# A searched order written anew: first fills on the rounded identity, first scores planned at half of TensorE's clock

## The chip, the cores and the metric

The kernel runs on one core of a Trainium2 chip. The metric is the device time of one execution in microseconds (us). Before the change it is 619.45 us, the median of three runs (618.64 to 619.97 us).

## The reference

Eight batches, eight heads, 576 positions, head dimension 64. Attention is causal by blocks of 64 positions; its output, 512 wide, goes through a gated feed-forward network with a convolution of three taps along the sequence:

```python
scores = scale * np.matmul(q, k.transpose(0, 1, 3, 2))
scores = np.where(block_i >= block_j, scores, -1000000000.0)
scores = scores - np.max(scores, axis=-1, keepdims=True)
attn = np.exp(scores)
attn = attn / (np.sum(attn, axis=-1, keepdims=True) + 1e-09)
x = np.matmul(attn, v)                    # heads side by side: (8, 576, 512)
h = np.maximum(x @ w_in, 0.0)             # w_in 512 x 1024
conv_out[s] = sum over k of conv_w[k] * h[s + k - 1]
out = (h / (1.0 + np.exp(-conv_out))) @ w_out   # w_out 1024 x 512
```

## The kernel before

The work is built as a list of 3694 operations (`Plan.op`, the class `Plan`), each with an engine, a planned duration, dependencies and buffers, and in some cases other engines on which it may run (`other`). `Plan.order` (L278) then makes the instruction streams. The list `TARGETS` (L21) has one number x per operation: x // 4 is its place on its engine, x % 4 picks one of the engines that it may run on (0 is the first). The operations of each engine are sorted by place; an engine issues its operations in that order and each waits for what it needs, on the chip as in the plan. The plan also gives every operation a start, by planned costs, and two things follow from those starts: which of the eight PSUM banks an operation gets, and where TensorE gets fills. A fill (`work`, L1767; the matmuls are line L1774) is a run of matmuls with a 128x512 result that nothing reads; the plan puts as many of them as fit where TensorE would be idle for more than 0.4 us. `speed` in `order` gives the factor on a TensorE duration, 1.0 at the full clock and 2.0 at half, by the work that the plan placed just before.

The first batch is done in pieces, because the weights arrive meanwhile. Its four head pairs first do queries 0 to 255 (part A: `stage_sa`, scores L1333, mask L1337, row maxima on VectorE L1351, exponentials on ScalarE L1359, norm on GpSimd L1374), then queries 256 to 575 (part B: `stage_sb`, scores L1272, mask L1276, maxima L1288, exponentials L1291; `last_s`, L1120, L1126). The attention weights are turned by TensorE (L1407, copies L677) and multiplied with v (L1451). A feed-forward pass (`ffn`) follows each part: input products L1544, relu L1563 or L1566, taps L1569, L1573, L1577, gate L1589, L1592, two fp16 planes L1599 and L1603, output products L1637, L1647.

The network's weights come as 64-bit words and are decoded, 512 KB at a time, sixteen times: L882 (ScalarE), L885 (GpSimd or VectorE), L889, L892, L897 (VectorE), the maximum L920, and a split into two fp16 planes, L952 and L960 (`wih`, `wil`, `woh`, `wol`).

From the second batch on a head pair goes through `stage_s` (scores L1108, maxima L1207, exponentials L1210), `two_planes` (L1053: the normed weights as a high and a low fp16 plane, L1057, L1063, L1067, L1073, L1079, on VectorE, ScalarE or GpSimd), three or four transposes by DMA (`xbar`, L1095, on SP's queue), and `pair_pv` (products with v, L1491, evacuation L1496, L1499, L1502).

At the start, the constant `rident` (L643, an identity rounded to fp32r) is made on VectorE from `ident`, `blank` (L664) is a 128x128 tile of zeros, and the other constants are made on ScalarE (L647). The first fill multiplies `blank`, all later ones `rident`. `scale_q` (L1015 on GpSimd, L1018 on ScalarE) scales q as it arrives. In the plan TensorE is free from 1.1 us on.

```python
        x = rident if len(fills) > 1 else blank
            return 1.0 if full else 2.0
```

Of the kernel before, what the change touches and what calls it, by code (L numbers as in the profile page):

```python
# [18 lines left out]
PE, DVE, ACT, POOL, SP = 0, 1, 2, 3, 4  # L19

TARGETS = """  # L21
# [199 lines left out]
class Plan:  # L221
# [56 lines left out]
    def order(self, targets, fill, clock):  # L278
        work, slots, unit, least, spare = fill
        step, up, down, begin, switch = clock  # L280
        used, full, known, rows = {}, False, 0, False
# [37 lines left out]
        free = [1.1, 0.0, 0.0, 0.0, 0.75]  # L319
# [1548 lines left out]
```

## Time and profile before

| | |
|---|---|
| three runs, us | 618.64, 619.45, 619.97 |
| profiled execution, us | 621.78 |
| its span, us | 619.9 |
| PE, DVE, ACT, POOL busy, us | 597.5, 530.7, 481.6, 386.9 |
| mean granted TensorE clock | 0.997 |
| fills (L1774) | 89 matmuls, 24.8 us on `rident` and 2.5 us on `blank` |

The span is the time from the first to the last instruction of the profiled execution; 1.88 us lie around it. Matmuls are pipelined and their durations overlap, so "busy" on PE counts the time in which at least one is under way. Fills count as busy. A stage's rows say more than the shares of the whole: the engines have different loads in the first 160 us and after.

### The profile page before, as it was taken

The page shows a single profiled execution, that of the slowest core. Times are in us where ns is not written, and L with a number is a line of the kernel's source. Part 1 is how long each engine was busy: PE and PEld are TensorE (multiplying, and loading weights), DVE is VectorE, ACT ScalarE, POOL GpSimd, SP SyncE. Part 2 cuts the span into 40 slices and gives each one's busy share as a digit, 9 for nine tenths or more (in the row PEclk, how much of TensorE's full clock was granted, in tenths as well). Part 3 has the DMA queues.
Part 4 walks back from the last instruction along what each step waited for, and adds up shares of the span by engine and source line. Part 5 has one row for each costly group of instructions (what it writes and reads, how often), then busy time and mean ns, then how long its engine had stood idle before and what let it go on. Part 6 is the DMA issues. An engine that isn't in the chain of part 4 may idle for free.

```text
span 619.9 us, 15505 instructions
## 1 busy us (share of the span) xinstructions
PE 597.5 (96%) x5832; PEld 381.2 (61%) x5832; DVE 530.7 (86%) x1122; ACT 481.6 (78%) x1234; POOL 386.9 (62%) x496
## 2 busy tenths in 40 slices
PE   8998899979999999999999999999999999999997
PEld 5556454447765477655775567555765667566754
DVE  5999999999889988999999998889889966973850
ACT  5999997796798659997799767978888857962721
POOL 4876665664495846986597454787786617852440
PEclk9999999999999999999999999999999999999999
DMA  8584412799938997699997699459886880594002
GB/s 296 206 293 146 139 35 92 170 224 192 255 78 217 195 221 129 139 196 218 198 189 139 143 223 227 110 116 209 188 172 117 195 145 18 108 163 120 1 1 86
DMA packets 205503, 97.77 MB, mean 158 GB/s; under 512 B 185308, under 2 KB 187636, under 8 KB 205428
## 3 DMA queue, kind: packets, MB, share of 16 engines
q1 hardware_dynamic: 203556, 93.63, 67.1%
q10 hardware_dynamic: 1872, 3.15, 1.8%
q8 instruction: 46, 0.75, 0.5%
q14 instruction: 29, 0.24, 0.1%
HBM read 41.44 MB, written 9.44 MB: 82 GB/s over the span
## 4 chain that ended last, share of the span: by engine, by line
PE 62%; DVE 25%; ACT 6%; POOL 3%; issue 2%; DMA 2%; DVEq 0%; ACTq 0%; POOLq 0%
PE banks L1637 22%; PE banks L1544 21%; PE banks L1491 8%; PE banks L1108 8%; DVE su L1207 3%; DVE t L1573 2%; PE banks L1774 2%; DVE ptbm L1063 2%; DVE t L1592 1%; DVE shared L897 1%; DVE ptbl L1063 1%; DVE st L1288 1%; DVE shared L892 1%; DVE vb L831 1%; DVE h L1063 1%
## 5 line engine op out<-in xcount | busy, mean ns | idle before, releaser
L1637 PE MATMUL banks<-woh,shared 128*128 128x512 f16 (+1 forms) x592 | 184.8, 374 | 0.3 <-DVE t L1592 0.3
L1544 PE MATMUL banks<-x,wih 128*128 128x288 f16 (+2 forms) x1024 | 156.7, 286 | 2.0 <-DVE t L1592 1.8
L1637 PEld LDWEIGHTS <-shared 128*128 128x128 f16 x888 | 82.7, 98 | 100.7 <-issue 15.0
L1544 PEld LDWEIGHTS <-wih 128*128 128x128 f16 x1024 | 98.0, 98 | 36.5 <-issue 8.6
L1207 DVE TENSOR_REDUCE su<-banks 128x1 f32<-128x192 f32 (+8 forms) x252 | 110.8, 478 | 3.1 <-PE banks L1108 2.2
L1637 PE MATMUL banks<-wol,shared 128*128 128x512 f16 (+1 forms) x296 | 110.5, 373 | 0.0
L1586 POOL TENSOR_TENSOR t<-t,shared 128x575 f32<-128x575 f32 x51 | 74.8, 1468 | 54.1 <-DVE t L1573 46.7
L1603 POOL TENSOR_TENSOR shared<-t,shared 128x576 f16<-128x576 f32 (+2 forms) x59 | 71.8, 1219 | 26.0 <-DVE shared L1599 12.8
L1544 PE MATMUL banks<-x,wil 128*128 128x288 f16 (+2 forms) x512 | 86.3, 286 | 0.6 <-DVE wil L960 0.6
L1108 PE MATMUL banks<-k,q 64*64 64x192 f32 (+9 forms) x1120 | 82.7, 414 | 3.9 <-DVE t L1592 1.1
L1491 PEld LDWEIGHTS <-vb 128*64 128x64 f16 x1848 | 63.0, 113 | 11.6 <-issue 10.9
L1573 DVE SCALAR_TENSOR_TENSOR t<-banks,cwb,t 128x575 f32<-128x575 f32 (+2 forms) x72 | 53.0, 742 | 12.5 <-ACT t L1569 7.5
L1108 PEld LDWEIGHTS banks<-k,q 64*64 64x64 f32 x1120 | 42.5, 132 | 33.9 <-issue 12.1
L1589 ACT ACTIVATE t<-t 128x576 f32<-128x576 f32 (+2 forms) x72 | 45.1, 629 | 23.1 <-POOL t L1586 16.5
L1544 PEld LDWEIGHTS <-wil 128*128 128x128 f16 x512 | 49.3, 98 | 14.9 <-DVE wil L960 1.2
L1592 DVE SCALAR_TENSOR_TENSOR t<-t,banks 128x576 f32<-128x576 f32 (+2 forms) x72 | 48.7, 680 | 8.4 <-ACT t L1589 7.6
L1569 ACT ACTIVATE t<-banks,cwb 128x576 f32<-128x576 f32 (+2 forms) x72 | 49.0, 684 | 6.6 <-DVE banks L1566 5.2
L1563 ACT ACTIVATE banks<-banks 128x576 f32<-128x576 f32 (+2 forms) x53 | 30.2, 574 | 15.8 <-PE banks L1544 15.4
L1210 ACT ACTIVATE p3f<-banks,su 128x512 f32<-128x512 f32 (+1 forms) x56 | 36.7, 659 | 5.5 <-DVE su L1207 2.2
L1582 ACT ACTIVATE shared<-banks,cwb 128x575 f32<-128x575 f32 x51 | 37.6, 738 | 1.9 <-DVE t L1573 0.8
L1647 ACT ACTIVATE stage<-banks,osc 128x512 f32<-128x512 f32 (+1 forms) x29 | 19.3, 668 | 24.7 <-PE banks L1637 24.7
L1210 ACT ACTIVATE p2f<-banks,su 128x384 f32<-128x384 f32 (+1 forms) x56 | 30.8, 552 | 8.3 <-DVE su L1207 4.4
(206 smaller groups left out, 1186.9 us busy)
## 6 DMA issues: line engine op xcount, KB each, us to landing
k<-in_k_dram SPq DMA_DIRECT2D x28, 368.0 KB, 3.7
vn<-in_v_dram SPq DMA_DIRECT2D x32, 320.0 KB, 3.9
q<-in_q_dram SPq DMA_DIRECT2D x28, 320.0 KB, 3.7
out_dram<-stage SPq DMA_DIRECT2D x24, 256.0 KB, 2.9
shared<-in_moe_w_in_dram SPq DMA_DIRECT2D x8, 512.0 KB, 4.1
shared<-in_moe_w_out_dram SPq DMA_DIRECT2D x8, 512.0 KB, 3.7
out_dram<-stage ACTq DMA_DIRECT2D x11, 256.0 KB, 3.7
k<-in_k_dram SPq DMA_DIRECT2D x4, 240.0 KB, 4.8
```

The source lines that it names most:

```text
L1108: nc.tensor.matmul(out[64 * y:64 * y + 64], t["q"].ap[64 * r:64 * r + 64, q0:q0 + 64], t["k"].ap[64 * r:64 * r + 64, k0:k0 + c1 - c0], sta ...
L1207: nc.vector.tensor_reduce(out=st.ap[:, k:k + 1], in_=home[hh].ap[:, x], op=ALU.max, axis=AX.X, negate=True)
L1210: nc.scalar.activation(out=y.ap[:, 0:n], in_=home[hh].ap[:, x], func=AF.Exp, bias=st.ap[:, k:k + 1], accum_out=st.ap[:, 9 + k:10 + k])
L1491: nc.tensor.matmul(y, vb.ap[:, w, c, j, :], x, start=first, stop=(z == 1 and c == jobs[-1][0]), skip_group_check=True)
L1544: nc.tensor.matmul(h(a, z), wt[:, c, fs], xs[c][xi].ap[:, x0 + a:x0 + z], start=(n + c - c0 == 0), stop=(n + c - c0 == 3 * NCC - 1))
L1569: nc.scalar.activation(out=t.ap[:, 0:no], in_=h(own, own + no), func=AF.Copy, scale=cwb.ap[:, NFC + f:NFC + f + 1])
L1573: nc.vector.scalar_tensor_tensor(out=t.ap[:, i0:no], in0=h(own + i0 - 1, own + no - 1), scalar=cwb.ap[:, f:f + 1], in1=t.ap[:, i0:no], op0 ...
L1586: nc.gpsimd.tensor_tensor(out=t.ap[:, 0:i1], in0=t.ap[:, 0:i1], in1=u.ap[:, 0:i1], op=ALU.add)
L1589: nc.scalar.activation(out=t.ap[:, 0:no], in_=t.ap[:, 0:no], func=AF.Tanh)
L1592: nc.vector.scalar_tensor_tensor(out=t.ap[:, 0:no], in0=t.ap[:, 0:no], scalar=1.0, in1=h(own, own + no), op0=ALU.add, op1=ALU.mult)
L1603: eng.tensor_tensor(out=g[1][:, f, carry:carry + no], in0=t.ap[:, 0:no], in1=g[0][:, f, carry:carry + no], op=ALU.subtract)
L1637: nc.tensor.matmul(fb.ap[:, 0:cut], g[a][:, f, cs], w[:, f, ds], start=(f == 0 and n == 0), stop=(f == NFC - 1 and n == 2))
```

## The change

`TARGETS` is replaced: all 3694 numbers are written anew; 283 operations get another engine than before, the rest another place or the same. The first fill multiplies `rident` like all others. In the plan alone, which decides bank numbers and fills, TensorE is free from 1.9 us instead of 1.1, `rounded_identity` costs 1.9 us instead of 2.45, everything that starts on TensorE up to 8.5 us has the factor 2.0 of half the clock, and the first three `stage_sa` score operations have a planned duration of 0.95 us for each of their two tiles instead of 0.405, before that factor. `firstk`, which nothing used, becomes `cold`, which counts these operations.

```diff
 TARGETS = """
-0 0 4 8 16 0 4 24 28 12 16 44 64 52 129 80 196 92 185 88 181 252 140 104 280 288 448 8 12 9 4 12 16 8 40 13 32 36 20 64 44 52 44 56 96 40 200 60 60 88
...
+0 4 8 16 0 0 4 24 28 12 20 44 76 52 181 72 240 104 185 96 193 268 152 108 288 296 388 8 20 28 4 8 12 12 44 14 32 40 16 36 32 40 32 40 88 36 184 48 93
...
+    COLD = 8.5
+
     def order(self, targets, fill, clock):
...
-            return 1.0 if full else 2.0
+            return 1.0 if full and t > self.COLD else 2.0
...
-        free = [1.1, 0.0, 0.0, 0.0, 0.75]
+        free = [1.9, 0.0, 0.0, 0.0, 0.75]
...
-    kept, gate, firstk = {}, [], []
+    kept, gate, cold = {}, [], []
...
-    made = [pl.op(DVE, 2.45, rounded_identity, -80.0)]
+    made = [pl.op(DVE, 1.9, rounded_identity, -80.0)]
...
         o = None
+        cold.append(at)
         for tiles in ABLK:
-            o = pl.op(PE, (0.345 + 0.06 * APM) * len(tiles), mm(tiles), at, deps=ready[0] + ready[1] + [o] + made[:2],
+            o = pl.op(PE, (0.95 if len(cold) < 4 else 0.345 + 0.06 * APM) * len(tiles), mm(tiles), at, deps=ready[0] + ready[1] + [o] + made[:2],
...
-        x = rident if len(fills) > 1 else blank
+        x = rident
```

Sorted by engine and place, the new numbers read as follows at the start (old order in brackets). SP: q and k of pair 0, the taps, q of pair 2, a block of weights, k of pair 2, q and k of pair 1 (old: k of pair 2 before the weights). TensorE: scores of part A of pairs 0, 2 and 1, then the turn of the taps (old: the turn before the third scores). ScalarE scales the first q (old: GpSimd), GpSimd the q of pair 2 (old: ScalarE). VectorE, after the maxima of the first scores: shift, maximum and merge of the first weight block, and only then the maxima of the second scores (old: maxima of the second scores first); three more decoding steps of weight blocks 0 and 1 stand ahead of the first part B maximum. Up to the last plane operation that VectorE does for the fourth pair of the second batch, it has 342 operations instead of 352: of the twenty that are no longer among them eleven run on GpSimd, six on ScalarE and three come later; of the ten that are new there, eight were GpSimd's, one ScalarE's and one came later. TensorE changes between score, v-product and other matmul operations 182 times instead of 195: up to the product with v of that fourth pair 53 times instead of 61, after it 129 instead of 134. The position of that product in TensorE's order, the 220th operation, is the same.

## Rows read from the trace of the kernel before

**Rows 1.** Page, engines: busy us, share of the span, instructions

```profile
PE 597.5 (96%) x5832; PEld 381.2 (61%) x5832; DVE 530.7 (86%) x1122; ACT 481.6 (78%) x1234; POOL 386.9 (62%) x496
```

**Rows 2.** Windows: length, busy of PE, PEld, DVE, ACT, POOL; clock, DMA share, GB/s

```profile
14.00:60.00 46.00, 41.80 (x320) 27.52 (x317) 45.81 (x125) 45.69 (x133) 32.99 (x48) 1.00 0.65 228
100.00:137.00 37.00, 32.32 (x308) 16.30 (x298) 34.98 (x91) 30.14 (x89) 22.26 (x33) 1.00 0.68 150
137.00:160.00 23.00, 22.91 (x292) 18.28 (x293) 20.34 (x46) 14.14 (x47) 11.08 (x17) 0.93 1.17 234
160.00:340.00 180.00, 176.45 (x1822) 112.06 (x1820) 168.08 (x329) 153.72 (x388) 130.29 (x156) 1.00 0.84 176
```

**Rows 3.** Chain of waits, 14 to 60 us and 100 to 137 us, by line

```profile
by line: DVE shared L892 14.7%; DVE shared L897 14.2%; DVE st L1288 13.6%; DVE wil L960 11.2%; DVE wm L920 9.0%; DVE shared L889 8.5%; DVE st L1126 4.7%; DVE x L1461 4.5%; issue 3.6%; DVE st L1351 1.7%; DVE t L1577 1.7%; DVE t L1573 1.7%; D
by line: DVE su L1207 16.7%; DMA ptbx<-ptbl 13.7%; DVE ptbl L1063 7.0%; DVE ptbm L1063 6.8%; DVE t L1573 5.3%; DVE t L1592 4.9%; POOL shared L1603 4.3%; DVE h L1063 3.9%; DVE t L1577 2.8%; issue 2.7%; ACT t L1589 2.6%; ACT shared L1596 2.6%
```

**Rows 4.** Chain of waits, single pieces: start us, us, what

```profile
8.08 2.00 PE banks L1774 x4
11.94 0.88 PE banks L1774 x2
138.51 3.85 PE banks L1491 x66
142.36 3.40 PE banks L1774 x14
149.24 2.24 PE banks L1491 x66
157.30 2.26 PE banks L1491 x66
```

**Rows 5.** Timeline of PE, first 13 us: start, us, line [idle before <-releaser]

```profile
1.05 2.50 PE L1774 MATMUL banks<-blank 128*128 128x512 f32 x5 [1.05 <-DVE blank L664]
3.92 0.80 PE L1333 MATMUL banks<-k,q 64*128 64x128 f32 x4 [0.36 <-POOL h L1148]
5.94 0.80 PE L1333 MATMUL banks<-k,q 64*128 64x128 f32 x4
10.02 0.80 PE L1333 MATMUL banks<-k,q 64*128 64x128 f32 x4
12.96 1.13 PE L1272 MATMUL banks<-k,q 64*128 64x512 f32 x4
```

**Rows 6.** Timeline of DVE: maxima and one decoding step in the first 15 us

```profile
5.88 1.35 DVE L1351 TENSOR_REDUCE st<-banks 128x1 f32<-128x256 f32 x4 [0.79 <-PE banks L1337]
7.89 0.76 DVE L1351 TENSOR_REDUCE st<-banks 128x1 f32<-128x256 f32 x2 [0.67 <-PE banks L1337]
9.18 0.66 DVE L892 SCALAR_TENSOR_TENSOR shared<-shared 128x512 int32<-128x512 int32 x1
11.98 1.35 DVE L1351 TENSOR_REDUCE st<-banks 128x1 f32<-128x128 f32 x5 [1.34 <-PE banks L1337]
14.15 0.69 DVE L1288 TENSOR_REDUCE st<-banks 128x1 f32<-128x512 f32 x1 [0.49 <-PE banks L1276]
```

**Rows 7.** Timeline of POOL: the scaling of pair 1's q; and windows, 5 to 8 us

```profile
7.78 0.40 POOL L1015 TENSOR_SCALAR q<-q 128x256 f32<-128x256 f32 x1 [3.95 <-DMA q<-in_q_dram]
...
5.00:8.00 3.00, 2.90 (x19) 1.95 (x17) 1.44 (x6) 1.67 (x8) 0.22 (x1) 1.00 1.00 344
```

**Rows 8.** One line, L1603, 160 to 320 us: ns min/median/max, first and last start

```profile
L1603 POOL TENSOR_TENSOR shared<-t,shared x16: 1272/1282/1863, 171.5 to 319.3; 128x576 f16<-128x576 f32 x16
L1603 DVE TENSOR_TENSOR shared<-t,shared x3: 751/752/1530, 170.1 to 243.6; 128x576 f16<-128x576 f32 x3
```

**Rows 9.** Timeline of PE: output products, then scores

```profile
108.98 0.38 PE L1637 MATMUL banks<-wol,shared 128*128 128x512 f16 x1
109.20 0.38 PE L1637 MATMUL banks<-woh,shared 128*128 128x512 f16 x1
109.53 0.94 PE L1108 MATMUL banks<-k,q 64*64 64x416 f32 x12
```

228 rows, old and new, of the table TARGETS are left out of this document.

## The prediction

> **What bounds the kernel now.** I read the engines' busy shares first, then windows by stage, the chain of waits, and the timeline of the first 15 us. PE is busy 96% of the span [rows 1], but that covers two different kernels. From 160 to 340 us PE is busy 176.45 of 180 us: its own work bounds it, and 3.55 us are idle [rows 2]. Before 160 us PE has slack that the share hides, because fills count as busy. From 14 to 60 us VectorE is busy 45.81 of 46 us and ScalarE 45.69, GpSimd 32.99 [rows 2], and the chain is VectorE: the listed shares of its lines add up to 85% [rows 3]. From 100 to 137 us VectorE is still busy 34.98 of 37 us, but its listed lines carry only 47% of the chain; a transpose by DMA has 14%, the rest is mostly ScalarE and GpSimd [rows 2, 3]. From 137 to 160 us the chain goes through fills: 14 of them from 142.36 us are 3.40 us in which PE waits for planes [rows 4]. At the very front the chain runs on PE: scores, and 2.00 us of fills at 8.08 us, then 0.88 us at 11.94 us [rows 4].
>
> So time can be won before 160 us, where VectorE decides, and hardly after it.
>
> **The change part by part.** The sum is made against the profiled execution, 621.78 us with a span of 619.9; the median of the runs is 2.33 us below it, and I take the difference over unchanged, so the terms are subtracted from 619.45.
>
> *The front (term A).* The granted clock's column shows 1.00 here, but the durations do not: the first scores of parts A (four matmuls, 0.80 us) take the same at 3.92, 5.94 and 10.02 us, and a whole group is 2.0 us (3.92 to 5.94) or 1.92 us (10.02 to the fills at 11.94) [rows 4, 5]. That is half the speed, the 1.2 GHz level. From 12.96 us on the part B scores run as they do later, at 2.4 GHz. The new plan charges the first two groups 2 tiles x 0.95 x 2.0 = 3.8 us each, the old one less than 2; the truth lies at 1.9. The new list therefore keeps PE free of fills there, and puts weight decoding before the second maxima on VectorE.
>
> Events with these durations. The first scores start as before, since q and k of pair 0 are still first on SP; the scaling of the first q goes from GpSimd, where one takes 0.40 us [rows 7], to ScalarE, where I put it at the same; were it twice as long, everything here would be 0.4 us late. The weights now stand before k of pair 2. k of pair 2 becomes the transfer (128 KB) just before q of pair 1. GpSimd could scale that q at 7.78 us; at 344 GB/s 128 KB take 0.4 us [rows 7], so k lands near 7.3 us, and the second scores start there and not at 5.94 us: PE idles about 1.4 us. They end near 9.2 us. The third scores start then, without the 2.00 us of fills in front of them, and end near 11.2 us, 0.8 us before the 11.94 us of now.
>
> VectorE idles 0.79 + 0.67 + 1.34 + 0.49 = 3.3 us ahead of its first part B maximum now [rows 6]. With the new order it idles 0.95 us before the first maxima (one decoding step has gone to GpSimd), then decodes for three steps from 7.2 to about 8.8 us (one is 0.66 us, a shift less [rows 6]), waits about 0.45 us for the second maxima (9.2 us) and 0.85 us for the third (11.2 us); after them three more decoding steps stand ready. That is 2.25 us idle, so A = 3.3 - 2.25 = 1.05 us; 85% of the chain up to 60 us is VectorE's, and I take 0.8 us. Bounds: if PE's clock rose later, two part B score groups (1.13 us for the longer [rows 5], taken for both) would double, 2.3 us; less the 0.8 us of head start this costs 1.5 us. If all idling went, 3.3 us would be won. The first fill on the identity instead of zeros and its later start cost nothing: PE waits for k at 3.92 us either way; the five zero fills ran from 1.05 to 3.55 us [rows 5].
>
> *VectorE up to the fourth pair's planes (term B).* Ten instructions fewer stand there. In the stretch 100 to 137 us one costs 34.98 / 91 = 0.384 us [rows 2], so 3.8 us. VectorE's listed lines hold 47% of the chain there, so 1.8 us of it reach the end; I take 1.7 us, since a plane that GpSimd makes is slower: L1603 takes it 1.28 us against VectorE's 0.75 [rows 8]. GpSimd gets three of the ten (net) and is busy 22.26 of 37 us; ScalarE gets five and is busy 30.14 [rows 2]: both have room. If that room fails, B is 0; if all of it counts, 3.8 us.
>
> Some VectorE instructions are held up by GpSimd: the same L1603 takes 751 ns, or up to 1530 [rows 8]. The Trainium skill (SBUF — State Buffer, "Who interferes with whom") says that GpSimd and a VectorE instruction with two SBUF inputs exclude each other for a whole instruction; by that rule three more instructions on GpSimd cost VectorE up to 3 x 0.78 = 2.3 us and B falls to 1.5 us of VectorE's time, 0.7 us of the end. The row agrees that it happens, not how often, so I leave B.
>
> *Order of PE after the fourth pair (term C).* Going from output products to scores costs 109.53 - 109.20 = 0.33 us where two output products are 0.22 us apart [rows 9]: 0.11 us. Five changes fewer make 0.55 us. The eight fewer before it lie in PE's slack and count nothing. What else the new order does to the 3.55 us of idling I put at 0; it may take all of it away or add as much. SP and the two moved output stores add nothing to PE.
>
> *Fills.* A fill takes time only where the plan foresaw less idling than there is; their number follows from the new plan's starts, which no list shows. Cover for them is PE's slack up to 157 us. If they grow, the v-products behind them are late by 0.24 us for each at full speed (3.40 us for 14) and 0.5 us at half (2.00 us for four) [rows 4].
>
> Sum: 0.8 + 1.7 + 0.55 = 3.05; 619.45 - 3.05 = 616.4 us.
>
> **The rivals.**
> *Hidden by the transposes.* From 137 to 160 us the DMA engines' mean share is 1.17 [rows 2]: the transposes of four pairs stand in a row, so planes that are ready sooner may only queue. For it: a transpose has 14% of the chain before. Against: the same stretch has VectorE on 20.34 of 23 us. B goes, and part of A: 619.45 - 0.4 - 0.55 = 618.5 us.
> *The clock falls back (slower).* From 137 to 160 us the granted clock is 0.93, and one group of v-products takes 3.85 us instead of 2.24 [rows 2, 4]: 1.6 us lost at the 1.2 GHz level, just after PE had idled in the waits before it. If the new plan, with other fills, leaves PE idle before the other three groups too, this costs 4.8 us, and the scores between them some 2.5 us: 616.4 + 7.3 = 623.7 us. It outweighs the gain from two more slow groups on (3.2 us against 3.05). The Trainium skill (TensorE: Matmul & The Clock Gate, "What's actually happening") has half rate as the state at rest, which activity lifts; the 0.93 agrees. For it: the plan's idea of the front is wrong by twice 1.9 us. Against: it places fills wherever it sees idling over 0.4 us.
> *The front does not do what it says.* The scores are charged 3.8 us and take 1.9, so the order that hides behind them is an order for another front: A is nothing, 617.2 us.
> *More is won after 160 us.* The 3.55 us of idling from 160 to 340 us go for the most part: 2.9 us more, 613.5 us.
>
> **How the numbers follow.** Forecast 616.4 us (own range 614.8 to 618.0): 0.42. Hidden 0.17, clock 0.11, front 0.16, more won 0.14. What a measurement can tell from no change is about 0.2%, 1.24 us: 618.2 to 620.7 us is "same". Faster: 0.42 + 0.14 + 0.12 of the front rival = 0.68. Same: 0.17 + 0.04 = 0.21. Slower: 0.11. The range reaches from 612.8 us (the last rival with a little of A's bound) to 620.4 us (A's loss of 1.5 us, no B, and C); the clock rival and tails are left out.
>
> **What would show it.** A: the second scores start near 7.3 us and the third end near 11.2 us, no fills between; VectorE's first L1288 comes after three more decoding steps and not later than about 14.5 us. B: the fourth pair's v-products (157.30 us now [rows 4]) start near 154.8 us, VectorE's busy time in 100 to 137 us no higher. C: from there to the end 0.5 us less. Wrong would be: part B scores at double duration, a granted clock well under 0.93 between 120 and 160 us, or the v-products of that pair at 157.3 us or later.

## The result, and the profile after

The changed kernel takes 628.65 us (median of 4 runs, 627.42 to 629.92); beside it the kernel before took 619.71 us. The ratio is 1.0136, 95% interval 1.0115 to 1.0158: slower by 8.4 us by the ratio, where I had forecast 3 us less. The profiled execution took 629.92 us with a span of 628.1.

Page, engines, of the kernel after, in the form of [rows 1]:

```profile
PE 602.1 (96%) x5843; PEld 384.4 (61%) x5843; DVE 532.6 (85%) x1129; ACT 485.8 (77%) x1236; POOL 383.5 (61%) x487
```

No engine has much more to do: TensorE 4.6 us more, mostly in slower scores at the front (its fills take 28.3 us instead of 27.3), ScalarE 4.2 and VectorE 1.9. So this is a loss by waiting, and the windows (columns as in [rows 2]) show where to look:

```profile
14.00:60.00 46.00, 41.59 (x317) 27.32 (x314) 43.37 (x119) 43.33 (x124) 33.17 (x45) 1.00 0.65 224
100.00:137.00 37.00, 35.19 (x285) 18.95 (x285) 32.52 (x79) 28.74 (x85) 19.99 (x31) 1.00 0.64 147
137.00:160.00 23.00, 20.72 (x272) 16.01 (x267) 20.36 (x48) 17.07 (x51) 9.86 (x16) 1.00 0.94 168
160.00:340.00 180.00, 176.94 (x1871) 114.74 (x1870) 165.30 (x330) 150.47 (x374) 129.02 (x154) 1.00 0.83 180
```

VectorE was busy 45.81 us from 14 to 60 us and is now busy 43.37, and 32.52 instead of 34.98 us from 100 to 137. After 160 us TensorE is as full as before. Most of the loss lies ahead of 160 us, in both of the stretches in which VectorE had decided. The granted clock is 1.00 from 137 to 160 us (0.93 before).

The front, timeline of PE (start, duration, line, idle before it), answering [rows 5]:

```profile
2.63 1.65 PE L1777 MATMUL banks<-rident 128*128 128x512 f32 x3 [2.63 <-DVE rident L645]
7.62 0.80 PE L1335 MATMUL banks<-k,q 64*128 64x128 f32 x4 [1.49 <-DMA k<-in_k_dram]
9.32 0.81 PE L1335 MATMUL banks<-k,q 64*128 64x128 f32 x4
12.69 2.08 PE L1274 MATMUL banks<-k,q 64*128 64x512 f32 x4
14.63 1.63 PE L1274 MATMUL banks<-k,q 64*128 64x384 f32 x4
16.24 1.56 PE L1122 MATMUL banks<-k,q 64*64 64x416 f32 x8
```

TensorE's events of part A are those that I forecast. But the part B scores take 2.08 us instead of 1.13: the 1.2 GHz level lasts until about 17.7 us, with 3 fills in the first 13 us where there had been 11.

The second place is where the first pair's v-products begin. First their start in the kernel before (timeline of PE, L1491), then the chain of waits after, from 133 to 137 us, and the fourth pair's v-products (start, duration, what):

```profile
129.23 1.07 PE L1491 MATMUL banks<-ptbx,vb 128*64 128x256 f16 x20
```

```profile
133.28 0.35 DVE ptbm L1081
133.71 0.56 ACT p1f L1212 x2
134.27 0.73 ACT p4f L1212 x2
135.05 2.32 PE banks L1494 x60
137.39 0.56 DVE vb L830
...
163.70 2.31 PE banks L1494 x60
```

The first pair's start at 135.05 us instead of 129.23, those of the fourth pair at 163.7 instead of 157.30 [rows 4]: 6.4 of the 8.2 us by which the two spans differ. What the first pair's wait for is neither their planes nor a transpose: it is ScalarE's exponentials (L1212), which read scores of other heads out of PSUM.

### The profile page after: what moved, and what is told of

Its sections match the earlier page's. It is cut to its first block, busy times and chain, and to the rows that moved or that the text cites. A ratio compares the mean times of both kernels' runs of the same rounds, so it can differ in the third digit from the quotient of the medians.

```text
span 628.1 us, 15552 instructions
## 1 busy us (share of the span) xinstructions
PE 602.1 (96%) x5843; PEld 384.4 (61%) x5843; DVE 532.6 (85%) x1129; ACT 485.8 (77%) x1236; POOL 383.5 (61%) x487
## 4 chain that ended last, share of the span: by engine, by line
PE 53%; DVE 26%; ACT 8%; POOL 6%; issue 3%; DMA 2%; SPq 1%; DVEq 0%; POOLq 0%; ACTq 0%
PE banks L1640 20%; PE banks L1547 17%; PE banks L1494 6%; PE banks L1110 6%; DVE su L1209 4%; DVE t L1576 3%; DVE t L1595 2%; DVE ptbm L1065 2%; DVE ptbl L1065 2%; DMA t<-h 2%; DVE vb L833 1%; POOL shared L1606 1%; DVE h L1065 1%; PE banks L1274 1%; POOL t L1589 1%
## 5 line engine op out<-in xcount | busy, mean ns | idle before, releaser
L1209 DVE TENSOR_REDUCE su<-banks 128x1 f32<-128x64 f32 (+8 forms) x252 | 110.6, 479 | 5.3 <-PE banks L1110 4.5
L1110 PE MATMUL banks<-k,q 64*64 64x256 f32 (+9 forms) x1120 | 82.5, 413 | 0.6 <-ACT ptbh L679 0.2
L1592 ACT ACTIVATE t<-t 128x576 f32<-128x576 f32 (+2 forms) x72 | 45.2, 629 | 27.1 <-POOL t L1589 17.5
L1595 DVE SCALAR_TENSOR_TENSOR t<-t,banks 128x576 f32<-128x576 f32 (+2 forms) x72 | 48.9, 681 | 11.0 <-ACT t L1592 10.1
L1566 ACT ACTIVATE banks<-banks 128x576 f32<-128x576 f32 (+2 forms) x57 | 32.7, 577 | 12.9 <-PE banks L1547 12.6
L1212 ACT ACTIVATE p3f<-banks,su 128x512 f32<-128x512 f32 (+1 forms) x56 | 36.8, 659 | 3.3 <-DVE su L1209 2.1
L1212 ACT ACTIVATE p2f<-banks,su 128x384 f32<-128x384 f32 (+1 forms) x56 | 30.8, 551 | 5.1 <-DVE ptbl L1065 2.3
L1777 PE MATMUL banks<-rident 128*128 128x512 f32 x100 | 28.3, 423 | 6.4 <-ACT p3f L1212 2.8
```

The source lines that it names most:

```text
L1110: nc.tensor.matmul(out[64 * y:64 * y + 64], t["q"].ap[64 * r:64 * r + 64, q0:q0 + 64], t["k"].ap[64 * r:64 * r + 64, k0:k0 + c1 - c0], sta ...
L1209: nc.vector.tensor_reduce(out=st.ap[:, k:k + 1], in_=home[hh].ap[:, x], op=ALU.max, axis=AX.X, negate=True)
L1212: nc.scalar.activation(out=y.ap[:, 0:n], in_=home[hh].ap[:, x], func=AF.Exp, bias=st.ap[:, k:k + 1], accum_out=st.ap[:, 9 + k:10 + k])
L1592: nc.scalar.activation(out=t.ap[:, 0:no], in_=t.ap[:, 0:no], func=AF.Tanh)
L1595: nc.vector.scalar_tensor_tensor(out=t.ap[:, 0:no], in0=t.ap[:, 0:no], scalar=1.0, in1=h(own, own + no), op0=ALU.add, op1=ALU.mult)
```

## The experiments

They ran in three groups (e1 to e4, e5 to e8, e9 to e12), each beside its own runs of the kernel before on the same chip (medians 620.21, 619.60 and 620.55 us); the ratios are against those. Each version has 4 to 12 runs.

**e1.** New list of places, all of the plan code as before.

```diff
-    COLD = 8.5
...
-        free = [1.9, 0.0, 0.0, 0.0, 0.75]
+        free = [1.1, 0.0, 0.0, 0.0, 0.75]
...
-            o = pl.op(PE, (0.95 if len(cold) < 4 else 0.345 + 0.06 * APM) * len(tiles), mm(tiles), at, ...
+            o = pl.op(PE, (0.345 + 0.06 * APM) * len(tiles), mm(tiles), at, ...
...
-        x = rident
+        x = rident if len(fills) > 1 else blank
```

> The new list of places with the old plan code (TensorE free from 1.1 us, identity 2.45 us, scores charged 0.405 us a tile, no cold start, first fill on zeros). The engines' orders are those of the changed kernel; the plan gives 43 fills between the fourth pair's first scores and its v-products (the changed kernel has 70 there: 2+22+7+8+16+10+5) and 16 fills in the first 13 us (changed kernel: 3). Theory FILLS (the 27 more fills at 0.24 us = 6.5 us push the v-products back): 620 to 623 us without a cold front mattering. Theory COLD (the missing fills at the front leave TensorE at 1.2 GHz until 17.7 us, and those 2 to 3 us are carried to the end): 625 to 626 us. Both together: 617 to 620 us. Theory ORDER (the new places themselves are worse): 627 to 630 us.

Measured: 622.46 us, ratio 1.0035 (1.002 to 1.005), in the range of FILLS, which e3 then tests. Three quarters of the loss goes with a few constants of the plan, although every engine still does the new list in the new order. About 2.2 us remain with the order and the banks that the old plan gives it.

**e2.** The changed kernel with the cold start of the plan taken out.

```diff
-    COLD = 8.5
+    COLD = 0.0
```

> The changed kernel with COLD = 0 alone: the same orders, the same banks as e1, 43 fills as in e1 before the fourth pair's v-products, but only 3 + 2 + 1 fills in the first 13 us. FILLS: 620 to 623 us, with the front as cold as in the changed kernel. COLD: 627 to 629 us. ORDER: 627 to 630 us. If both hold, this is 2 to 3 us above e1. That banks make the difference can't be told from FILLS here (e3 does that).

Measured: 623.67 us, 1.0044 (1.0027 to 1.0061), a little above the range of FILLS. One number in the plan is worth 0.9% of the kernel, with the front nearly as bare of fills as in the changed kernel. What that number alters in the program is fills and the PSUM banks of 400 of 2011 operations, nothing else.

**e3.** The changed kernel with 27 fills fewer, all else kept.

```diff
         fills.append(k)
+        n = {8: 0, 9: 12, 12: 6, 14: 0}.get(len(fills) - 1, k)
...
-            for _ in range(k):
+            for _ in range(n):
```

> The changed kernel, its plan, orders and banks unchanged; only the fills before the v-products are cut to those of e1 (22 to 12, 16 to 6, and 2 and 5 to none: 27 fewer). FILLS: 622 to 623 us (27 x 0.24 = 6.5 us less). COLD, ORDER, and a theory BANKS (400 operations on other banks wait for them): 627 to 630 us, or more if TensorE goes to 1.2 GHz in the idle time that the fills covered.

Measured: 629.34 us, 1.0147 (1.0128 to 1.0166). My theory FILLS falls. Without them the wait that they had covered stands open in the timeline of PE:

```profile
128.29 3.01 PE L1778 MATMUL banks<-rident 128*128 128x512 f32 x12 [1.11 <-ACT p3f L1212]
133.68 1.07 PE L1494 MATMUL banks<-ptbx,vb 128*64 128x256 f16 x20 [2.38 <-ACT p4f L1212]
154.44 1.07 PE L1494 MATMUL banks<-ptbx,vb 128*64 128x256 f16 x20 [3.03 <-ACT p4f L1212]
```

TensorE stands still for 2.38 and 3.03 us ahead of the v-products of the first and third pair, until ScalarE has read p4f's scores. The waits of VectorE (what waited for what: us in total, times, longest) from 116 to 165 us show who pays:

```profile
DVE vb L830 <- PE banks L1494: 5.3, 2, 2.8
DVE su L1232 <- ACT su L1229: 0.6, 1, 0.6
```

VectorE cannot split the next v (L830) until those v-products have read the old one, and its maxima are queued behind that split. So a late release of one pair of banks comes back to the engine that the stage depends on.

**e4.** The changed kernel with fills at the front: five on zeros from 1.1 us, three behind the first scores, two behind the third.

```diff
-        free = [1.9, 0.0, 0.0, 0.0, 0.75]
+        free = [1.1, 0.0, 0.0, 0.0, 0.75]
...
+            more = {201: 3, 224: 2}.get(o.seq, 0)
+            if more:
+                x = Op()
+                x.eng, x.fn, x.start, x.end = PE, work(0, more), o.start + 1e-6, o.start + 2e-6
+                done.append(x)
...
-        x = rident
+        x = rident if len(fills) > 1 else blank
```

> The changed kernel with fills at the front as before the change: the first fills on zeros from 1.1 us, 3 more fills while TensorE waits for the second k (1.49 us idle at 6.1 us) and 2 after the third scores; nothing else. COLD: TensorE at 2.4 GHz from about 13 us on, VectorE 2 us earlier from 25 us on, 625.5 to 627 us. FILLS, ORDER, BANKS: 627.5 to 630 us, although the front is up to 1 us earlier.

Measured: 627.69 us, 1.0115 (1.009 to 1.014). That is not in COLD's range but in that of the other theories. The front itself goes as COLD says, here in the timeline of PE:

```profile
5.22 0.97 PE L1782 MATMUL banks<-rident 128*128 128x512 f32 x3
11.20 1.13 PE L1279 MATMUL banks<-k,q 64*128 64x512 f32 x4
132.90 1.07 PE L1499 MATMUL banks<-ptbx,vb 128*64 128x256 f16 x20 [0.30 <-ACT p4f L1217]
```

The part B scores come 1.5 us earlier and at full speed, and the first v-products start at 132.9 us instead of 135.05. By the ratios 1.3 us of it reach the end, but the two intervals overlap; e12 repeats it.

**e5.** The changed kernel with one score tile in another bank.

```diff
+                    if o.seq == 788 and b is o.banks[0]:
+                        z = 0
                     last[z] = b.tag
                     b.slot, tenant[z] = z, b
```

> The changed kernel, all of its orders and its plan code kept; one tile alone (operation 788, a score tile of the second batch half that the plan opens at 79 us of its own time) is put into PSUM bank 0 instead of 2, and the plan gives the later tiles their banks from there: 702 of 2011 operations get other banks. The front is that of the changed kernel to the instruction, the fills before the v-products are the 43 of e1 and, but for the place of the last ten, of e3. Theory BANKS (the changed plan spreads single-bank tiles so that tiles that need two neighbouring banks, the v-products of the first pair above all, wait for ScalarE to read old scores): the v-products start without the 2.4 us wait of e3, 623 to 624.5 us, 5 to 6 below e3's 629.34. Theories ORDER and COLD: 627.5 to 630 us as e3.

Measured: 623.56 us, 1.0064 (1.0037 to 1.0091), apart from e3's interval: 0.83%, 5.1 us, from one tile's bank and what follows from it. The same places in the timeline of PE as in e3:

```profile
128.58 3.02 PE L1779 MATMUL banks<-rident 128*128 128x512 f32 x12 [1.27 <-ACT p3f L1214]
131.53 1.07 PE L1496 MATMUL banks<-ptbx,vb 128*64 128x256 f16 x20
149.32 1.29 PE L1496 MATMUL banks<-ptbx,vb 128*64 128x256 f16 x20
```

Both waits are gone. The third pair, which e3 reached at 154.44 us, starts at 149.32. A v-product tile and a score tile of 576 columns each take two neighbouring banks (`two_banks`). The plan hands out the eight banks one tile at a time, in the order of its own start times. Once those shift, single-bank tiles fall so that no free pair is left but the one whose scores ScalarE reads last. The Trainium skill (Perfetto Trace Analysis, "Matmuls") advises independent matmul groups to rotate through different PSUM banks, so that one group is read out while the next is made; the 2.38 and 3.03 us of e3 are what it costs here where that rotation fails.

**e6.** The kernel before with the same tile moved, for the other direction.

```diff
+                    if o.seq == 788 and b is o.banks[0]:
+                        z = 6
```

> The kernel before, nothing of the change in it, with the same tile (operation 788, opened at 75 us by its plan) put into bank 6 instead of 3; 406 operations get other banks, the orders stay, the fills before the v-products go from 42 to 49. BANKS: the same kind of wait can be made in the old order, 623.5 to 625.5 us, the first v-products 3 to 4.5 us late. If banks are no cause of their own and the new order was needed for the wait: 620 to 621 us.

Measured: 622.19 us, 1.0039 (1.0016 to 1.0062). Slower, by 2.4 us, less than I expected. Timelines of PE and of ACT:

```profile
127.39 4.15 PE L1776 MATMUL banks<-rident 128*128 128x512 f32 x17 [0.87 <-ACT p3f L1212]
131.47 1.07 PE L1493 MATMUL banks<-ptbx,vb 128*64 128x256 f16 x20
```

```profile
131.02 0.47 ACT L1212 ACTIVATE p1f<-banks,su 128x256 f32<-128x256 f32 x1
```

The v-products of the first pair start at 131.47 us, against 126.74 in e8, which has the old banks and order up to there; about 1.1 of these 4.7 us had been lost before 117 us. They begin as ScalarE's p1f ends (131.49) and as 17 fills end, where there had been 5. So one tile's bank costs time in the old order as well, about half as much, but this trace doesn't tell the wait for the banks from the fills that the plan puts before it (49 for 43 in that stretch).

**e7.** Old plan code, the new order until 175 us, the old one behind.

```diff
 TARGETS = """
...  (operations that e1's plan starts before 175 us: new places and engines; all others: old, behind them)
```

> Old plan code; the new order and engines for the 1245 operations that the plan of e1 starts before 175 us, the old order for all behind them. e1 was 2.2 us slower than before with an order that is new throughout. Theory LATE (its loss is in the feed-forward stage, where TensorE waits 0.9 us twice between 420 and 460 us for VectorE): 619 to 620.5 us, the gain or tie of the first stage alone. Theory EARLY (the new front with the second k behind the weights, and more done by GpSimd, costs what the rest gains): 621.5 to 623 us. My forecast's terms A and B, had they been right for the order alone, would give 617 to 618.5 us.

Measured: 620.45 us, 1.0012 (0.9994 to 1.0031). That is in LATE's range, and not the 617 to 618.5 us of my terms A and B. The timeline of DVE, around two maxima over all rows:

```profile
32.12 0.29 DVE L722 TENSOR_REDUCE vs<-banks 128x1 f32<-128x128 f32 x1 [0.59 <-PE banks L719]
42.65 0.29 DVE L722 TENSOR_REDUCE wm<-banks 128x1 f32<-128x128 f32 x1 [0.58 <-PE banks L719]
```

and the windows of 14 to 60 us, e7 and then e8:

```profile
14.00:60.00 46.00, 40.51 (x318) 27.52 (x310) 44.73 (x123) 44.46 (x127) 35.70 (x47) 1.00 0.66 231
```

```profile
14.00:60.00 46.00, 42.22 (x327) 28.49 (x326) 45.96 (x126) 45.68 (x130) 33.98 (x49) 1.00 0.69 236
```

The new order has VectorE read each maximum too soon. GpSimd has still to spread it (TensorE waits 1.14 and 1.05 us for dg, L715), TensorE to turn it, and VectorE idles 0.59 + 0.58 us of its 46, ahead of the two lines above.

**e8.** The mirror of e7: the old order until 175 us.

```diff
 TARGETS = """
...  (operations that before's plan starts before 175 us: old places and engines; all others: new, behind them)
```

> The mirror of e7: old plan code, the old order for the 1239 operations that the plan of before starts before 175 us, the new order and engines behind them. LATE: 621.5 to 623 us. EARLY: 619.5 to 620.5 us. Term C of the forecast alone: 619.7 us.

Measured: 620.82 us, 1.0023 (1.0 to 1.0045): between the two ranges, nearer to EARLY's 620.5 than to LATE's 621.5. The two halves of the order (0.12% and 0.23%) add up to e1's 0.35%, but neither is clear of no change, so where the order loses is not shown. The run showed more by its front, where it has the instructions of the kernel before (timeline of PE):

```profile
3.48 0.80 PE L1333 MATMUL banks<-k,q 64*128 64x128 f32 x4
4.91 0.47 PE L1333 MATMUL banks<-k,q 64*128 64x128 f32 x4
8.95 0.49 PE L1333 MATMUL banks<-k,q 64*128 64x128 f32 x4 [1.71 <-POOL q L1015]
10.81 1.13 PE L1272 MATMUL banks<-k,q 64*128 64x512 f32 x4
```

The second scores take 0.47 us and not 0.80, and the part B scores come at 10.81 us and not at 12.96 [rows 5]. VectorE is 2.2 us earlier from 20 to 120 us. The execution that I had read for before was late at its front.

**e9.** e7 with VectorE's two early reads put one instruction later.

```diff
+        for x, y in ((24, 78), (101, 93)):
+            self.ops[x].start = self.ops[y].start + 1e-6
         done.sort(key=lambda o: o.start)
```

> e7 (new order until 175 us, old plan code) with two pairs of neighbouring VectorE instructions exchanged: the two maxima over all rows that read what TensorE and GpSimd have made (0.29 us) come after the decoding step that now follows them (0.68 us). In e7 VectorE, ScalarE and TensorE all stand still there for 0.58 and 0.59 us, which the old order (e8) does not show. Theory READS (the new order loses its first 1.2 us there): 619.2 to 619.8 us, VectorE idle 14 to 60 us at most 0.2 us. If GpSimd's work ahead of them is the limit anyway (the dg tile is 1.05 us late for TensorE): 620.2 to 620.8 us, the idle time moves to TensorE and ScalarE alone.

Measured: 620.16 us, 0.9998 (0.9982 to 1.0013). VectorE's idle time there is gone but for 0.28 us (45.72 us busy of 46; READS said at most 0.2). The time lies between the two ranges, 0.14% under e7's; the intervals overlap, so READS is neither shown nor refuted.

**e10.** The first edit alone on the kernel before.

```diff
-        x = rident if len(fills) > 1 else blank
+        x = rident
```

> The kernel before with the first edit alone: the five first fills multiply the identity, so they start when VectorE has made it (about 2 to 2.6 us) and not at 1.05 us; plan and order unchanged. Theory COLD (TensorE reaches 2.4 GHz later when it starts later, and the first scores stand behind the fills): the first scores start at 4.5 to 5 us, 620.5 to 622 us. If the front has slack for it: 619.3 to 620.2 us, within the measurement of no change.

Measured: 619.90 us, 0.9994 (0.9981 to 1.0008), no difference. The first scores start at 4.37 us, but the third start at 8.80 us all the same (8.95 in e8, where TensorE waits 1.71 us for q). The front has the slack for a later start.

**e11.** Six zero fills instead of five at the start of the kernel before.

```diff
+        n = k + (len(fills) == 1)
...
-            for _ in range(k):
+            for _ in range(n):
```

> The kernel before with six zero fills at the start for five, nothing else. In the execution that my forecast was read from TensorE idled 0.36 us before the first scores and stayed at 1.2 GHz until 12.5 us; in e6 and e8, the same instructions until then, it idled 0.08 us or nothing and was at 2.4 GHz from 4.7 us on, and VectorE was 2.2 us earlier. If that idle time decides which of the two an execution gets, the sixth fill (0.5 us, ends at 4.05 us) closes it: 618.5 to 619.3 us and less spread. If chance or something else decides: 619.6 to 620.2 us, since the first scores come up to 0.5 us later.

Measured: 620.46 us, 1.0006 (0.9993 to 1.002), no difference. Here too the third scores wait for q (1.41 us) and start at 8.62 us. The idle time before the first scores is closed and full speed is there from 3.9 us on (0.51 us for the first scores), but the time is not 618.5 to 619.3 us. What decides when the clock rises in one execution was not settled: e4 had full speed by 5.2 us (3 fills in 0.97 us), e12 with the same instructions there not before 9 us, here in its timeline of PE:

```profile
5.53 1.65 PE L1784 MATMUL banks<-rident 128*128 128x512 f32 x3
```

**e12.** The edits of e4 and e5 together.

```diff
+            more = {201: 3, 224: 2}.get(o.seq, 0)
...
+                    if o.seq == 788 and b is o.banks[0]:
+                        z = 0
```

> The changed kernel with the one bank of e5 and the front fills of e4 together. If the causes add up (e5 took 5.8 us off e3, e4 1 us off the changed kernel): 622 to 622.8 us, what e1 has with all of the old plan code. If the front is only worth something while the later waits hide it: 623.3 to 624 us.

Measured: 622.14 us, 1.0042 (1.0021 to 1.0062). They add up: 0.22% below e5, as e4 was 0.21% below the changed kernel.

So the loss of 1.36% is banks 0.83% (5.1 us, e3 against e5), order 0.35% (2.2 us, e1, with the banks that the old plan gives it) and the bare front 0.21% (1.3 us, e4 and e12): 1.39%. The banks are shown by intervals that lie apart, and so is the order as a whole, by an interval clear of no change, though not where it loses; the front rests on two small differences that agree. No version tried is faster than the kernel before: e9 and e10 are level with it.

## Why the prediction was wrong, by its own steps

**What bounds the kernel.** Right in the main: 6.4 of the 8.2 us between the spans were lost ahead of the fourth pair's v-products, 1.8 behind them. One reading was not right: the 14 fills at 142.36 us stand ahead of input products (L1544, 145.61 us), which need the x that VectorE finishes at 145.42 us (L1502), and not ahead of v-products.

**What the plan constants do: the step that failed.** The paragraph *Fills* takes them as bearing on fills alone ("their number follows from the new plan's starts"), and the sum has no term for them. But the plan that counts the fills also gives every PSUM tile its bank, and that is the largest term, 5.1 us. It was in no term, no bound and no rival: e3's trace has TensorE wait 2.38 and 3.03 us for a pair of banks that ScalarE still reads, and e5 takes both waits away. It could have been looked for: the prediction names the v-products' planes and transposes as what they wait for, and never asks what has to leave the bank that they are written to. The plan itself had the size: in its own planned time, which both kernels work out without the chip, `Plan.order` ends the last operation at 612.2 us in the changed kernel and at 606.8 us in e5, 5.4 us apart (before: 603.7 us). It is no guide to the order, though: for e1 it ends at 602.0 us, and e1 is slower than before.

**Fills.** They did grow, from 43 to 70 between 116 us and the fourth pair's v-products. The priced 0.24 us each did not follow: 27 of them taken out gave nothing (e3). They filled a wait.

**Term A.** TensorE's events were right (7.62 us for 7.3, 11.18 for 11.2, no fills between), its sign was not. VectorE's first part B maximum comes at 14.85 us, and the idle time ahead of it is 1.56 + 0.65 + 0.43 + 0.54 = 3.18 us where I had put 2.25 (timeline of DVE, its last piece):

```profile
14.85 1.29 DVE L1290 TENSOR_REDUCE st<-banks 128x1 f32<-128x512 f32 x2 [0.54 <-PE banks L1278]
```

The bound that I gave for a later clock, 1.5 us lost, is near what came, 1.3 us, with the part B scores at double duration that I had named as what would make it wrong. That the sizes agree is partly luck: the bound takes 2.3 us for the slower scores and 0.8 us of head start, where the two groups take 0.95 + 0.71 us more and start 0.27 us earlier. The base was off too: I charged the old front 3.3 us of idle VectorE from one execution and left the 2.33 us between it and the median "unchanged", while in e8 the same instructions put VectorE's first part B maximum at 12.01 us instead of 14.15 [rows 6]. Of the three executions with these instructions (before, e6, e8) two have the early front.

**Term B.** No run shows the ten instructions fewer bring the fourth pair forward. With the new order its v-products start at 156.1 us (e1), 155.2 (e7) and 153.5 (e9), with the old one at 153.5 (e8), 155.6 (e10) and 156.0 (e11). Counting instructions of a full engine assumes that it stays full; the new order made it wait 1.17 us at two reads (e7). e9 takes nearly all of that away and only draws level with e8, so beyond these waits it stays open why the 1.7 us did not come.

**Term C.** Not to be seen. e8, which has the new order behind 175 us, is level or slower. In the changed kernel, in e1 and in e8 TensorE waits 1.6 us in two pieces for VectorE's t (L1595, L1592 in e1 and e8) after 340 us, where before it waits 0.5 us once. Whether this is the 1.2 us by which e8's median lies higher was not tried.

**The rivals.** "The clock falls back" had the right sign and the wrong place: from 137 to 160 us the granted clock is 1.00. "The front does not do what it says" is right that A is not won. The other two had the sign wrong, as the forecast had. None had the banks. 620.4 us as the upper end came from adding up priced terms, with nothing kept for what the plan decides unseen.

## What to carry to other kernels

When a planner writes out a kernel, its cost constants are part of the program: one that is meant for the first 8 us renumbers buffers at 120 us. Look at what a tile waits for to be free, not only at what feeds it, above all for tiles that need two neighbouring banks. And read a second execution of the kernel before pricing a stretch as short as the front; if the profiled one is 2.3 us above the median, ask in which stage.

## What the runs showed that I had not expected

The same instructions at the front reached 2.4 GHz at about 4.7 us in one execution (e8) and at about 12.5 us in another (before). How much of those 2.2 us reaches the end is open: e11, at full speed from 3.9 us on, has its part B scores 2.5 us before those of [rows 5], but its first v-products 1.2 us and its end only 0.4 us earlier. In both the column of the granted clock reads 1.00 for these microseconds; only the durations tell. And one tile's bank number, with the banks that follow from it, moves 5.1 us in an engine order that is otherwise the same (e3 against e5).
